# One VectorE product for both spectra in the FFT batches of an S4 and GEGLU layer, with a new order table

## The chip, the cores and the metric

The kernel runs on one core of one Trainium2 chip. The metric is the device time of one execution in microseconds (us). The time before is the median of three runs. In what follows PE is the matrix engine (TensorE) and PEld its weight loads, DVE is VectorE, ACT is ScalarE, POOL is GpSimd, SP is SyncE, which issues most DMAs.

## The reference, cut to what matters

```python
def _A_ref(u, A_re, A_im, B_re, B_im, C_re, C_im, log_dt, Dskip):
    ...
    P = jnp.exp(logdA[:, :, None] * l[None, None, :])
    K = jnp.einsum("dn,dnl,dn->dl", Cc, P, dB).real      # 448 channels, 256 states, 2048 steps
    ...
    Yf = Uf * Kf[None, :, :, :]                          # spectra of u and of K, length 4096
    y = irfft2(Yf)[..., :L]
    return y + u * Dskip

mod = (silu(c) @ w_mod)                                  # six rows: sa, ca, ga, sb, cb, gb
h = layernorm(x) * (1 + ca) + sa
x = x + ga * _A_ref(h, ...)
h = layernorm(x) * (1 + cb) + sb
x = x + gb * ((gelu(h @ w_gate) * (h @ w_up)) @ w_down)  # 448 -> 1792 -> 448
```

All inputs and the output are float32. The part that the change touches is the product of the two spectra.

## The kernel before, in words

The work falls into two halves. The first half makes the convolution kernel K, transforms u and K, multiplies the spectra and transforms back. The second half is the gated feed-forward network, in four blocks of 512 tokens.

**Making K.** The 448 channels are taken eight at a time, in 56 steps. For a step, PE makes the arguments of exponentials and of sine and cosine in PSUM (tile pg: `x.mm` line 639, `y.mm` line 658, `ang` and `anc` line 676). ACT evaluates them (`x.exp` line 645 into mx, `y.exp` line 663 into my, `mag` line 681, `sin` line 689, `cos` lines 693 and 700, into fg). DVE multiplies them into two factor tiles (`tx` line 722, 1024 elements per partition; `tyc` line 726, 2048 elements). PE contracts the factors (`kgen`, line 749, 64 small matmuls into kg). For each pair of steps `kev` copies the result out (tile ke), `kd` (line 767) adds the skip term, `ka` (line 772) does the first FFT stage, and `kout` copies that into the tile ako. `mag`, `kev`, `kout` and several other copies may be on ACT or on DVE; the order table says which for each instance. Copies on ACT have line 481, those on DVE line 483.

**The transform of u.** Four blocks of u are loaded (xt), normalised (`bn`, `norm`, `as`) and go through the first stage on PE (`ua`, line 922) to DRAM (u_d), then through the second stage (`ub`, line 985, evacuated by `ub.eg`, line 993, or `ub.ev` to tile uo) and back to DRAM (us). This runs beside the making of K.

**The product.** The channels are in three groups of 160, 160 and 128. For each of the first two groups `k_fft` runs eleven batches of three frequencies. A batch loads the spectrum of u in two arrangements into one tile (`f.ut`: ut[:, 0] is the spectrum itself, ut[:, 1] has its real and imaginary halves swapped; three DMAs, lines 1086 and 1088), loads the Fourier matrices (`f.fc`, tile fc), makes the batch's K spectrum in PSUM (`f.fwd`, line 1093, 3 matmuls of 160 columns), multiplies both arrangements by it (`f.pr`, line 1097, two operations of 3 x 160 = 480 elements each), transforms back (`f.inv`, line 1104, 6 matmuls per batch), copies out (`f.z`) and stores (`f.st`). The inverse takes the two products of a frequency in two adjacent matmuls. The third group goes through `t_fft`, with products on lines 1196 and 1199, once K is complete.

**The order.** Nothing is scheduled at run time. Every step is a task with a name and a running number, and the table PLACE gives each task one place in a single list of 2006; a letter behind a place names the engine or queue where there is a choice (a ACT, d DVE, p POOL, s SP). `Plan.run` issues the tasks in that list's order, so the table sets the order of every engine's instruction queue and of every DMA queue. Each engine works through its queue strictly in order.

The start is a chain of its own: `sil2` (lines 796 to 798) turns c into silu(c), `m.ld` loads rows of w_mod (line 806, tile fg), `m.mm` (line 816) and `m.mq0` (line 812) multiply them on PE, and the scale row for the normalisation of u (gs, line 860) needs two of them.

Of the kernel before, what the change touches and what calls it, by code (L numbers as in the profile page):

```python
# [40 lines left out]
    "anc": "127 138 148 162 173 210 218 246 266 319 327 332 359 351 433 450 484 460 499 483",  # L41
    "ang": "110 113 140 158 168 164 207 221 247 312 323 331 347 350 423 444 459 448 498 476 508 584 615 595 665 680 663 703 "
        "747 763 768 791 795 815 782 883 889 928 904 914 938 946 1012 1028 1019 1040 1045 1054 1116 1133 1142 1148 1163 "
        "1169 1175 1196",
    "as": "65d 58d 80d 105d 115d 120d 156a 146d 254d 252d 282d 296d 321a 317a 341a 353a",
    "bn": "20 45 24 40 15 17 48 16 215 216 238 245 157 220 194 190",
    "c.ai": "133",
    "c.ak": "231",
    "c.au": "47",
    "c.c": "8",  # L50
    "c.ea": "57",
    "c.ih": "516",
    "c.ld": "4",
    "c.rd": "51",
    "c.t1": "363",
    "co.adde": "1339 1352 1355 1360",
    "co.addl": "1380 1385 1420 1414",
    "co.addx": "1495 1510 1499 1522 1672 1712 1735 1684 1791 1803 1809 1801",
    "co.ca": "1400a 1406a 1446a 1439a",
    "co.cb": "1417a 1418d 1452d 1453a",  # L60
    "co.h0": "1393d 1404a 1432d 1435a",
    "co.h2": "1534a 1580a 1571a 1562a 1748a 1744d 1755a 1760d 1848d 1882a 1833a 1866a",
    "co.l0": "1408 1411 1437 1447",
    "co.l2": "1541 1585 1573 1577 1749 1751 1757 1761 1849 1885 1843 1876",
    "co.mme": "1322 1340 1335 1349",
    "co.mml": "1374 1379 1384 1387",
    "co.mmx": "1492 1506 1494 1509 1636 1699 1731 1645 1784 1797 1804 1788",
    "co.n": "1392 1403 1430 1425",
    "co.nx": "1527 1575 1549 1532 1745 1742 1747 1759 1821 1868 1829 1863",
    "co.rc": "1391 1402 1429 1424",  # L70
    "co.rcx": "1525 1739 1820",
    "co.rt": "1381 1386 1428 1422",
    "co.rtx": "1524 1737 1810",
    "co.xt": "1542 1586 1574 1578 1750 1752 1758 1762 1850 1886 1851 1877",
    "co.ta": "1398 1405 1434 1438",
    "co.tb": "1409 1415 1449 1448",
    "cos": "522 592 638 616 672 699 700 712 762 776 789 814 808 819 796 894 910 942 907 922 945 952 1016 1037 1022 1048 1060 "
        "1068 1127 1137 1153 1160 1172 1183 1207 1229",
    "cos2": "128 141 152 163 178 211 219 253 272 320 328 343 360 354 440 451 490 467 505 488",
# [3 lines left out]
    "d0": "172",  # L83
# [21 lines left out]
    "dsk": "174",  # L105
    "dt": "5",
# [4 lines left out]
    "ev.end": "1249",  # L111
    "ev.fp": "715",
    "ev.geg": "1462",
    "ev.pq": "1334",
    "ev.ps": "1433",
    "ev.ub": "397",
    "ev.w0": "1337",
    "f.fc": "724 731 767 790 810 850 871 877 918 950 964 1027 1056 1071 1098 1112 1146 1124 1202 1203",
    "f.fwd": "746 759 787 820 825 856 884 908 936 951 967 1008 1023 1039 1057 1073 1101 1126 1156 1145 1217 1214",
    "f.inv": "756 780 800 823 843 867 911 919 940 966 992 1014 1034 1051 1066 1094 1114 1131 1184 1173 1228 1225",  # L120
    "f.pr": "748 766 788 821 842 866 888 909 939 961 980 1009 1024 1043 1065 1082 1104 1130 1174 1168 1224 1221",
    "f.st": "774 827 826 891 875 901 977 960 976 997 995 1072 1062 1079 1103 1119 1121 1177 1226 1216 1260 1272",
    "f.ut": "720 758 771 794 824 855 872 899 935 916 958 993 1002 1038 1046 1070 1083 1106 1155 1115 1179 1192",
    "f.z": "757a 781a 809a 835a 869a 895d 912a 920a 965d 996a 994d 1017d 1035a 1063d 1089a 1095a 1120a 1132a 1208a 1201a "
        "1248d 1237a",
    "gs": "66 86",
# [27 lines left out]
        "1141a 1167a 1195a 1222a 1244a 1247a",  # L154
    "lt0": "64 144 325 368 560 801 861 985",
    "lt1": "92 195 326 369 723 802 968 986",
    "m.cp": "581a 600d 786a",
    "m.cp0": "50d",
    "m.ev": "44 60 63 589 619 804",
    "m.ld": "29 31 30 420 578 760",  # L160
# [251 lines left out]
def s4_geglu(ctx: ExitStack, tc: tile.TileContext, a: dict, out: bass.AP):  # L412
# [39 lines left out]
    dt, dt2 = dts_[:, :4], dts_[:, 4:]  # L452
# [1381 lines left out]
```

## Time and profile before

| | before |
|---|---|
| device time, median of 3 runs | 777.25 us (776.79 to 779.4) |
| device time of the profiled execution | 776.06 us |
| its span, first to last instruction | 774.3 us |
| granted TensorE clock | 0.995 |
| PE busy | 724.2 us (94%) |
| DVE busy | 591.3 us (76%) |
| ACT busy | 459.7 us (59%) |
| DMA traffic | 139.87 MB, mean 181 GB/s |

The span is divided into an opening of some 20 us, the making of K and the transforms up to about 340 us, a passage of some 40 us in which the third group is transformed back, and the feed-forward network from 381 us to the end. An engine's share over the whole span mixes these stages, so the busy time is read stage by stage. A row of the groups gives line, engine, operation, output <- input with shapes, count, then the summed busy time in us and the mean of one in ns, then the idle time of that engine just before them and what ended it. A row of the timeline gives the start and the length in us; the time in brackets is idle time before it.

### The profile page before, as it was taken

To read this page: it belongs to the slowest core of one execution; us is meant where nothing else is said; L and a number is where in the kernel's file an instruction comes from. 1 tells how busy PE (TensorE), PEld (TensorE's weight loads), DVE (VectorE), ACT (ScalarE), POOL (GpSimd) and SP (SyncE) were. 2 spreads that over 40 slices of the span, in tenths; PEclk is the share of its full clock that TensorE was granted. 3 is DMA by queue.
4 is the path that set the end of the run, shared out by engine and by line. 5 is a ranking of instruction groups with operands and counts; after the bars stand their busy time and mean duration, and the time that the engine had idled before them with its cause. 6 is when DMAs were issued, how large, how long until landed. Compare 5 with 4: busy or idle time off the path is not lost.

```text
span 774.3 us, 19010 instructions
## 1 busy us (share of the span) xinstructions
PE 724.2 (94%) x8166; PEld 442.5 (57%) x8166; DVE 591.3 (76%) x891; ACT 459.7 (59%) x613; POOL 8.5 (1%) x23
## 2 busy tenths in 40 slices
PE   2877889998899999989999999999999999999997
PEld 1333554443677777677874445444694446944487
DVE  6999999999999999979958932578774577144743
ACT  5899999999999999952646620244312433022330
POOL 0000000000000000003000000000000000000000
PEclk9999999999999999999999999999999999999999
DMA  9764777997888687897787791455247224013201
GB/s 265 193 187 160 214 184 222 276 272 236 247 230 252 180 233 239 275 310 208 235 269 257 221 235 79 146 166 211 98 82 211 96 96 136 14 50 99 77 2 60
DMA packets 103950, 139.87 MB, mean 181 GB/s; under 512 B 34388, under 2 KB 85492, under 8 KB 103866
## 3 DMA queue, kind: packets, MB, share of 16 engines
q1 hardware_dynamic: 100436, 132.53, 58.2%
q10 hardware_dynamic: 2950, 5.38, 2.0%
q8 instruction: 64, 1.05, 0.6%
q0 software_dynamic: 480, 0.75, 0.3%
q14 instruction: 20, 0.16, 0.1%
HBM read 100.39 MB, written 36.01 MB: 176 GB/s over the span
## 4 chain that ended last, share of the span: by engine, by line
PE 73%; ACT 12%; DVE 8%; DMA 4%; issue 2%; SPq 1%; DVEq 0%; ACTq 0%
PE pq L1530 32%; PE pq L1630 9%; PE pd L1599 4%; PE pg L676 4%; PE pf L1104 4%; PE kg L749 3%; ACT my L663 3%; DVE ty L726 2%; PE pq L1524 2%; PE pf L985 2%; PE pf L1093 2%; PE kg L772 2%; PE pf L1206 2%; ACT fg L689 2%; DMA us<-uo 2%
## 5 line engine op out<-in xcount | busy, mean ns | idle before, releaser
L1530 PE MATMUL pq<-ht,wr 128*128 128x512 f16 (+1 forms) x1200 | 248.3, 365 | 0.1
L1530 PEld LDWEIGHTS <-wr 128*128 128x128 f16 x1200 | 114.6, 98 | 128.5 <-issue 11.3
L726 DVE TENSOR_TENSOR ty<-my,fg 128x2048 f32<-128x2048 f32 x56 | 127.3, 2284 | 0.4 <-ACT fg L693 0.3
L1537 ACT ACTIVATE ge<-pq 128x512 f32<-128x512 f32 (+1 forms) x60 | 34.0, 566 | 106.9 <-PE pq L1524 71.3
L1544 DVE TENSOR_TENSOR fq<-ge,pq 128x512 f32<-128x512 f32 (+1 forms) x60 | 39.0, 650 | 72.6 <-PE pq L1530 45.0
L1556 ACT ACTIVATE hh<-fq 128x1024 f16<-128x1024 f32 (+1 forms) x49 | 46.7, 962 | 65.6 <-DVE fq L1544 47.0
L1630 PE MATMUL pq<-d,hh 128*128 128x224 f16 x476 | 68.9, 259 | 0.0
L722 DVE TENSOR_TENSOR tx<-mx,fg 128x1024 f32<-128x1024 f32 x56 | 67.6, 1218 | 0.2 <-ACT fg L700 0.2
L749 PE MATMUL kg<-ty,tx 128*32 128x64 f32 x3584 | 61.6, 222 | 4.4 <-DVE tx L722 1.7
L749 PEld LDWEIGHTS kg<-ty,tx 128*32 128x32 f32 x3584 | 53.2, 111 | 21.3 <-issue 5.9
L1559 DVE TENSOR_TENSOR hlo<-fq,hh 128x1024 f16<-128x1024 f32 (+1 forms) x49 | 53.7, 1106 | 12.9 <-ACT hh L1556 12.7
L1630 PE MATMUL pq<-d,hlo 128*128 128x224 f16 x238 | 61.6, 259 | 0.0
L689 ACT ACTIVATE fg<-pg 128x1024 f32<-128x1024 f32 x56 | 57.6, 1040 | 0.5 <-PE pg L676 0.3
L663 ACT ACTIVATE my<-pg 128x1024 f32<-128x1024 f32 x56 | 56.2, 1032 | 0.4
L1630 PEld LDWEIGHTS <-hh 128*128 128x128 f16 x560 | 54.1, 98 | 0.9 <-issue 0.2
L693 ACT ACTIVATE fg<-fg,small 128x1024 f32<-128x1024 f32 x36 | 42.2, 1180 | 0.0
L1104 PE MATMUL pf<-q,fc 128*128 128x160 f32 x264 | 41.5, 307 | 0.0
L1104 PEld LDWEIGHTS pf<-q,fc 128*128 128x128 f32 x264 | 36.5, 190 | 5.3 <-issue 2.2
L676 PEld LDWEIGHTS <-lt 64*128 64x128 bf16 x304 | 17.7, 95 | 35.0 <-issue 22.7
L676 PE MATMUL pg<-ea,lt 64*128 64x512 bf16 x152 | 31.3, 390 | 6.5 <-ACT fg L689 3.0
L1747 ACT ACTIVATE d<-fq 128x896 f16<-128x896 f32 x14 | 13.2, 946 | 39.7 <-PE pd L1599 27.3
L985 PE MATMUL pf<-ui,fu 128*128 128x448 f32 x66 | 31.2, 576 | 1.2 <-DVE uo L993 0.5
(210 smaller groups left out, 1119.2 us busy)
## 6 DMA issues: line engine op xcount, KB each, us to landing
wr<-w_d SPq DMA_DIRECT2D x21, 896.0 KB, 4.6
fc<-in_k_fc SPq DMA_DIRECT2D x20, 576.0 KB, 4.2
u_d<-so SPq DMA_DIRECT2D x32, 224.0 KB, 3.0
ui<-u_d SPq DMA_DIRECT2D x10, 672.0 KB, 6.0
fq<-in_wd SPq DMA_DIRECT2D x14, 448.0 KB, 4.1
w<-in_wgu SPq DMA_DIRECT2D x11, 512.0 KB, 4.6
us<-uo SPq DMA_DIRECT2D x22, 240.0 KB, 4.5
q<-us SPq DMA_DIRECT2D x22, 240.0 KB, 4.5
```

The costliest lines, as they stand in the source:

```text
L663: A.activation(yb.tile.rearrange("p h (n k) -> p n h k", n=2), pb.tile.rearrange("p (n h k) -> p n h k", n=2, h=2), AF.Exp)
L676: T.matmul(pa[:, nh * 512:nh * 512 + 512], w, x, start=(k == 0), stop=(k == 2))
L689: A.activation(fb.tile[:, 0].rearrange("p x (n k) -> p n x k", n=2), pb.tile.rearrange("p (n x k) -> p n x k", n=2, x=2), AF.Sin, scale=TW ...
L722: V.tensor_mul(tx.tile, xb.tile[:, xm, None, :].to_broadcast([128, 2, 512]), fb.tile[:, :, 0])
L726: V.tensor_mul(ty.tile, yb.tile[:, :, None, :].to_broadcast([128, 2, 2, 512]), fb.tile[:, None, :, 1].to_broadcast([128, 2, 2, 512]))
L749: T.matmul(kg[32 * g:32 * g + 32, 2 * (s % 2) + q, :64], tx[:, r, nh, 4 * q + g], ty[:, 0:4:3, nh, 4 * q + g] if r else ty[:, 1:3, nh, 4 * ...
L985: T.matmul(pb.tile, fu.tile[:, i], ui.tile[:, EORD[e0 + i] % 32 - s0], start=True, stop=True)
L1104: T.matmul(pz.tile[:, e % 32 - sl0], fc.tile[:, i, 1 + t], pp.tile[:, t, i], start=(t == 0 and e != 32), stop=(t == 1 and e != 0))
L1530: T.matmul(pb.tile[k][:, ts], wr.tile[:, 4 * lo + t, k, c0:c0 + 128], ht[:, m, ts], start=f % 2 == 0 and i == 0, stop=f % 2 == 1 and i == 9)
L1556: A.activation(hg.tile[0][:, cb, c], fq.tile[:, c], AF.Copy)
L1559: V.tensor_sub(hg.tile[1][:, cb, c], fq.tile[:, c], hg.tile[0][:, cb, c])
L1630: T.matmul(bank(k)[:, m], x[:, p, q[0], ts], w[:, p, q[1]], start=new and m == 0 and p == 0 and z == 0, skip_group_check=True, stop=i in ( ...
```

## The change

Line 1097 and its loop become one operation. It takes both arrangements of the spectrum of u (2 x 3 x 160 = 960 elements per partition) and reads the batch's K spectrum twice, through an access pattern that repeats it. There are 22 such batches.

```diff
         def prod():
-            for t in range(2):
-                V.tensor_mul(pp.tile[:, t, :ne], ut.tile[:, t, :ne], pk.tile[:, :ne])
+            V.tensor_mul(pp.tile[:, :, :ne], ut.tile[:, :, :ne], pk.tile[:, None, :ne].to_broadcast([128, 2, ne, n]))
```

The program is one line shorter from there on, so line 1097 becomes 1096, and every later line has a number one lower.

The rest of the change is a new table PLACE. Nearly every place up to about 1480 of the 2005 is different, most by less than ten places; the places of the feed-forward network behind it are as they were. The engine letters change too: of 16 `as` 14 instead of 11 are on DVE, of 28 `kev` 13 instead of 16, of 28 `kout` 6 instead of 7, of 36 `mag` 8 instead of 7, of 16 `ub.ev` 6 instead of 4, of 22 `f.z` 8 instead of 6, of 4 `p.e1` 4 instead of 3; the others of each are on ACT. Two lines of the table:

```diff
-    "f.pr": "748 766 788 821 842 866 888 909 939 961 980 1009 1024 1043 1065 1082 1104 1130 1174 1168 1224 1221",
+    "f.pr": "744 769 794 817 837 858 889 901 938 962 981 1004 1021 1041 1066 1076 1099 1123 1181 1148 1202 1209",
...
-    "kev": "199d 230d 290a 345a 378d 393a 462a 518d 548a 577a 654a 705a 735d 818d 805d 853d 897d 924d 969d 983d 1030d 1075d "
-        "1113d 1140a 1162a 1191a 1239d 1236a",
+    "kev": "209d 260a 290a 320a 390d 403d 420d 500a 545a 566d 683a 707a 724d 815d 799d 843a 893d 924a 971d 980a 1045d 1070d "
+        "1107a 1136a 1171a 1197a 1240d 1241a",
```

At the places that the prediction speaks of, the queues change as follows (a row of a queue gives line, operation, output <- input, size and how many follow one another; + and - mark rows of the new and of the old order). The first is SP's queue at the start of the program, where ld, c_sb, xt, fg and lh_d are the tiles that hold log_dt, c, a block of u, a row of w_mod and the scratch of the K parameters:

```order
 L487 DMA ld<-in_A_log_dt 112x4
+L512 DMA q<-in_abc 112x512
+L853 DMA xt<-in_A_u 128x1792
 L487 DMA c_sb<-in_c 112x4
-L853 DMA xt<-in_A_u 128x1792 x2
-L806 DMA fg<-in_w_mod 112x1792 x3
-L515 DMA lh_d<-in_k_one 224x512
+L806 DMA fg<-in_w_mod 112x1792 x2
+L853 DMA xt<-in_A_u 128x1792
+L515 DMA lh_d<-in_k_one 224x512
+L806 DMA fg<-in_w_mod 112x1792
```

The first two rows of w_mod now stand behind one block of u instead of two, and the third stands behind the second block.

The second is DVE's queue a little later, where the three operations of `sil2` make c_sb. Before:

```order
L549 TENSOR_TENSOR q<-q 112x256
L796 TENSOR_SCALAR sig<-sig 112x4
L797 RECIPROCAL sig<-sig 112x4
L798 TENSOR_TENSOR c_sb<-c_sb,sig 112x4
L557 TENSOR_TENSOR q<-q 112x256
```

And after:

```order
L579 TENSOR_TENSOR q<-q 112x256
L796 TENSOR_SCALAR sig<-sig 112x4
L797 RECIPROCAL sig<-sig 112x4
L798 TENSOR_TENSOR c_sb<-c_sb,sig 112x4
L583 SCALAR_TENSOR_TENSOR q<-q 112x256
L537 TENSOR_TENSOR q<-q,lh 112x512
L574 SCALAR_TENSOR_TENSOR q<-q 112x256
L575 RECIPROCAL q<-q 112x256
```

c_sb is now made behind line 579 and no longer ahead of line 557.

The third is the end of the making of K on DVE. Before:

```order
L726 TENSOR_TENSOR ty<-my,fg 128x2048
L722 TENSOR_TENSOR tx<-mx,fg 128x1024
L1097 TENSOR_TENSOR q<-q,pf 128x480 x4
L726 TENSOR_TENSOR ty<-my,fg 128x2048
L722 TENSOR_TENSOR tx<-mx,fg 128x1024
L483 COPY ke<-kg 128x4x63
L767 TENSOR_TENSOR ke<-kg,d_115 128x4 x2
L483 COPY zo<-pf 128x480
```

And after:

```order
L1096 TENSOR_TENSOR q<-q,pf 128x960
L722 TENSOR_TENSOR tx<-mx,fg 128x1024
L1096 TENSOR_TENSOR q<-q,pf 128x960
L722 TENSOR_TENSOR tx<-mx,fg 128x1024
L726 TENSOR_TENSOR ty<-my,fg 128x2048 x2
L722 TENSOR_TENSOR tx<-mx,fg 128x1024
L483 COPY ke<-kg 128x4x63
L767 TENSOR_TENSOR ke<-kg,d_115 128x4 x2
L483 COPY zo<-pf 128x320
```

The last product now has four factor operations behind it instead of two, and the last copy to zo on DVE has 320 elements instead of 480.

334 rows, old and new, of the table PLACE are left out of this document.

## The prediction

> **What bounds the kernel now.** I first read the cores and the busy time stage by stage (header, then one row per stretch of the span: PE, PEld, DVE, ACT and POOL busy with their instruction counts, the granted clock, the DMA share and rate).
>
> ```profile
> core 0: 774.3 us, clock 0.995
> ...
> core 0: us, PE busy (x) PEld busy (x) DVE busy (x) ACT busy (x) POOL busy (x), PEclk, DMA share, GB/s
> 0.00:20.00 20.00, 4.52 (x8) 2.23 (x8) 13.57 (x34) 11.22 (x19) 0.88 (x10) 1.00 0.91 266
> 20.00:60.00 40.00, 31.56 (x282) 13.62 (x280) 38.00 (x66) 37.35 (x50) 0.00 (x0) 0.96 0.72 195
> 60.00:200.00 140.00, 123.24 (x2186) 64.69 (x2184) 136.82 (x174) 137.44 (x183) 0.00 (x0) 0.99 0.78 224
> 200.00:340.00 140.00, 136.82 (x2726) 103.33 (x2726) 137.06 (x140) 133.19 (x154) 0.00 (x0) 1.00 0.82 241
> 340.00:381.00 41.00, 38.67 (x488) 32.67 (x489) 34.49 (x71) 15.97 (x34) 7.58 (x13) 1.00 0.74 218
> 381.00:774.00 393.00, 389.37 (x2482) 225.91 (x2480) 231.41 (x410) 124.49 (x177) 0.00 (x0) 1.00 0.44 134
> ```
>
> From 60 to 200 us DVE and ACT are both 98% busy and PE 88%. From 200 to 340, where the 22 batches run, PE and DVE are both 98% busy and ACT 95%. So no single engine can be relieved alone there: DVE has 3.2 us of idle time in the first of these stretches and 2.9 in the second. From 381 on PE is 99% busy and the order is nearly the old one, so the time is decided by when that stretch begins.
>
> Then DVE's waits between 60 and 345 us (waiting line, releaser, us in total, times, longest) and what the inverse transforms on PE waited for (us, times):
>
> ```profile
> DVE ke L767 <- ACT ke L481: 1.6, 2, 1.2
> DVE q L1097 <- PE pf L1093: 1.5, 3, 0.7
> ...
> DVE ty L726 <- ACT fg L693: 0.3, 1, 0.3
> ```
>
> ```profile
>   DVE q L1097: 1.5, 4
> ```
>
> All of these are small. DVE is held by its own work, with ACT and PE close behind.
>
> **The product.** The groups on DVE, and the pitch of operations that follow one another without a gap in the timeline (start, length):
>
> ```profile
> L726 DVE TENSOR_TENSOR ty<-my,fg 128x2048 f32<-128x2048 f32 x56 | 127.3, 2284 | 0.4 <-ACT fg L693 0.3
> L722 DVE TENSOR_TENSOR tx<-mx,fg 128x1024 f32<-128x1024 f32 x56 | 67.6, 1218 | 0.2 <-ACT fg L700 0.2
> ...
> L1097 DVE TENSOR_TENSOR q<-q,pf 128x480 f32<-128x480 f32 x44 | 26.5, 648 | 1.6 <-PE pf L1093 1.5
> ```
>
> ```profile
> 330.60 1.22 DVE L722 TENSOR_TENSOR tx<-mx,fg 128x1024 f32<-128x1024 f32 x1
> 331.74 2.29 DVE L726 TENSOR_TENSOR ty<-my,fg 128x2048 f32<-128x2048 f32 x1
> 333.94 1.22 DVE L722 TENSOR_TENSOR tx<-mx,fg 128x1024 f32<-128x1024 f32 x1
> 335.08 2.34 DVE L1097 TENSOR_TENSOR q<-q,pf 128x480 f32<-128x480 f32 x4
> 337.33 2.29 DVE L726 TENSOR_TENSOR ty<-my,fg 128x2048 f32<-128x2048 f32 x1
> 339.54 1.22 DVE L722 TENSOR_TENSOR tx<-mx,fg 128x1024 f32<-128x1024 f32 x1
> ```
>
> By the means, an element costs (1218 - 648) / 544 = 1.05 ns and an operation has a fixed part of 648 - 480 x 1.05 = 145 ns. But each operation starts 0.08 us before the one ahead of it ends (331.74 + 2.29 = 334.03, the next at 333.94), so that part is paid only in part. Four products take 337.33 - 335.08 = 2.25 us, 0.563 each; 1024 elements take 1.14, 2048 take 2.20, so an element costs (2.20 - 1.14) / 1024 = 1.035 ns. A product of 960 then takes 0.563 + 480 x 0.001035 = 1.06 against 1.125 for two: 0.065 us saved, times 22 batches = 1.4 us of DVE time. The bounds are 0 (the repeated read is no faster than two operations) and 22 x 0.145 = 3.2 (the whole fixed part). I take 1.4: the timeline has the pitch of this very operation, and the factor tile of line 726, which is built from two repeated reads, shows no extra price.
>
> The Trainium skill would put it higher. Its page Perfetto Trace Analysis (Optimizing Scalar/DVE Operations) gives a Vector instruction about 125 ns of overhead on PSUM, 60 on SBUF, and advises grouping when the engine is saturated; as an estimate from that page, 22 x 0.125 = 2.75 us. The pitch above, with one operand in PSUM, agrees with the lower figure, and the measurement decides. The page VectorE: DVE Perf Modes (The DRAIN you can't avoid) says that a next operation waits until the pipe is empty, by which the saving would be the upper bound; the starts above come before the end, so the trace speaks against it here.
>
> The merged operation must wait for all three loads of the batch and for the K spectrum at once; the next factor operations are queued behind it on DVE, and the inverse behind it on PE. The loads cost nothing: no DMA stands among the waits of line 1097. The inverse needs both products from its second matmul on, so its start moves by less than one product, 0.56, and only in the four batches where PE waited: at worst 4 x 0.56 = 2.2 us of PE waits, and I take 0, since the second half also ends 0.065 earlier.
>
> The Trainium skill has a rule against such merging in the same section of Perfetto Trace Analysis: where Vector isn't saturated but makes others wait, smaller instructions may finish work sooner. The trace has DVE at 98% there, so the rule's condition isn't met.
>
> **The moved copies.** The engine letters move work between ACT and DVE. Rows on DVE, then three of their counterparts on ACT:
>
> ```profile
> L684 DVE TENSOR_SCALAR fg<-pg 128x1024 int32<-128x1024 int32 x7 | 8.5, 1218 | 0.3 <-PE pg L676 0.3
> L483 DVE COPY ke<-kg 128x252 f32<-128x252 f32 x16 | 6.6, 412 | 0.6 <-PE kg L749 0.6
> L483 DVE COPY ako<-kg 128x512 f32<-128x512 f32 x7 | 4.8, 683 | 0.0
> L483 DVE COPY zo<-pf 128x480 f32<-128x480 f32 x6 | 3.9, 650 | 0.0
> L483 DVE CAST lh<-q 112x512 bf16<-112x512 f32 x9 | 3.8, 418 | 0.1
> L912 DVE TENSOR_SCALAR as<-au,rs 128x128 f32<-128x128 f32 x11 | 3.0, 281 | 0.2
> L483 DVE COPY uo<-pf 128x448 f32<-128x448 f32 x4 | 2.5, 620 | 0.2 <-DMA us<-uo 0.2
> ```
>
> ```profile
> L681 ACT ACTIVATE fg<-pg 128x1024 f32<-128x1024 f32 x29 | 30.2, 1044 | 0.1
> L481 ACT ACTIVATE ke<-kg 128x252 f32<-128x252 f32 x12 | 4.8, 404 | 5.1 <-PE kg L749 5.1
> L910 ACT ACTIVATE as<-au,rs 128x128 f32<-128x128 f32 x5 | 2.0, 400 | 0.0
> ```
>
> Each counted at its mean less the 0.08 overlap, and up to the last factor operation: DVE gains one `mag` (+1.14), three `as` (+0.60), one cast to lh (+0.34), two copies to uo (+1.08) and two of 480 to zo (+1.14; one stood behind the last factor before), and loses three to ke (-1.0) and one to ako (-0.6). That is +2.7 us, and with the merge DVE's work up to its last factor is 2.7 - 1.4 = +1.3 us. ACT's rows are about as long, so I take it as 2.7 us lighter. I count DVE's +1.3 in full, since DVE has almost no idle time, and set against it what ACT's relief can give back: DVE waits on ACT for about 2 us in the list above; I take 1.0 of it (bounds 0 and 2.7).
>
> **The opening.** SP's queue, PE's first matmul, the step that makes c_sb, the row that stood ahead of the new place of it, and the scale row that ends this chain on ACT; then the size of one block of u:
>
> ```profile
> 2.62 0.90 SPq L853 DMA_DIRECT2D xt<-in_A_u  x2
> 3.56 2.28 SPq L806 DMA_DIRECT2D fg<-in_w_mod  x3
> ```
>
> ```profile
> 15.48 4.97 PE L816 MATMUL pf<-fg,c_sb 112*128 112x448 f32 x8 [15.48 <-DVE q L574]
> ```
>
> ```profile
> 8.02 0.16 DVE L798 TENSOR_TENSOR c_sb<-c_sb,sig 112x4 f32<-112x4 f32 x1
> ...
> 13.16 0.43 DVE L579 TENSOR_TENSOR q<-q 112x256 f32<-112x256 f32 x1
> ```
>
> ```profile
> 24.58 0.54 ACT L834 ACTIVATE gs<-pf 128x448 f32<-128x448 f32 x1 [1.42 <-PE pf L816]
> ```
>
> ```profile
> xt<-in_A_u SPq DMA_DIRECT2D x4, 896.0 KB
> ```
>
> The first matmul names DVE as its releaser, but c_sb was done at 8.2; what came at 15.5 must be the first row of w_mod, which stood behind two blocks of u. One block less is 0.92 MB / 266 GB/s = 3.4 us sooner. Then c_sb is the later one: behind line 579 and its three short steps it is ready at about 13.16 + 0.35 + 0.5 = 14.0. So PE starts up to 1.4 us sooner. The scale row needs the third row of w_mod as well, whose place behind the same bytes is unchanged, so I take half, 0.7 (bounds 0 and 1.4).
>
> **The rest.** SP issues the same DMAs in another order; the passage from 340 to 381 has PE 94% busy with unchanged work, so I take 0 there, with 2.3 us (its PE idle time) as the bound to either side.
>
> The sum: +1.3 - 1.0 - 0.7 = -0.4 us against the profiled execution's own 776.06 (span 774.3 and 1.8 around it). The median of the runs is 1.2 above that execution, so the forecast for the median is 777.25 - 0.4 = 776.9. A measurement of this kernel can tell about 0.3%, 2.3 us, from no change.
>
> **The rivals.**
>
> Faster: ACT, not DVE, sets the pace up to 200 us. For it: ACT is the busiest there (137.44 of 140), and PE, 88% busy, would take up the batches as soon as they can start. Then ACT's 2.7 us come off in full, with 0.7 from the opening: 777.25 - 3.4 = 773.9. Against it: DVE has only 3.2 us of idle time there, and its own work grows.
>
> Slower: the ledger of DVE alone decides. The merged operation takes as long as two, ACT's relief and the opening give nothing, and the moved copies are paid in full: 777.25 + 2.7 = 780.0. It decides from a pitch of the merged operation of about 1.11 us on (2.7 less 22 x 0.015 is 2.3). For it: DVE's 98%. Against it: the pitches of lines 722 and 726.
>
> That the change doesn't do what it says can be left out: the new queue of DVE holds 22 operations of 960 elements and none of 480.
>
> **How the numbers follow.** The forecast, no measurable change, gets 0.42, the faster rival 0.32, the slower 0.26; a new order of some 1480 steps can lose or win small waits anywhere, which keeps the two rivals high. The range reaches past both: to 773.9 less the other half of the opening and as much of the passage (0.7 each), 772.5, and to 780.0 plus 1.0 of the PE waits priced above, 781.0.
>
> **What would show it.** In the profile after: line 1096 x22 with a mean near 1.14 us (1.06 and the overlap of 0.08) and a pitch of 1.06; DVE still 97% busy or more from 60 to 340 with ACT some 2 to 3 us lighter up to the last exponentials; PE's first matmul near 14; the last factor operation on DVE within 2 us of 339.5. The prediction is wrong if the last factor moves by more than 2.3 us, if line 1096 waits for DMAs, or if the passage of 41 us changes by more than 2.

## The result and the profile after

The changed kernel is slower. Over two sets of runs its median is 785.8 us (four runs, 782.6 to 790.1) and 784.2 us (six runs, 783.2 to 787.1), against 778.1 and 778.6 for the kernel before beside them: ratios 1.010 (95% interval 1.0068 to 1.0132) and 1.0081 (1.0062 to 1.0100). The prediction, 776.9 with a range of 772.5 to 781.0, is wrong in sign and size. The profiled execution took 784.24 us, with a span of 782.5 us, 8.2 more than before. The medians differ by less, 7.7 and 5.6 us; the profiled execution of the kernel before, 776.06, is faster than all four of its runs beside the changed kernel (776.79 to 779.4).

The same views as before, first the cores and the busy time by stretch:

```profile
core 0: 782.5 us, clock 0.993
...
0.00:20.00 20.00, 4.67 (x7) 2.21 (x8) 11.86 (x30) 10.88 (x18) 0.81 (x10) 1.00 0.92 228
20.00:60.00 40.00, 29.68 (x191) 12.29 (x190) 32.49 (x61) 31.35 (x42) 0.00 (x0) 0.87 0.64 180
60.00:200.00 140.00, 123.05 (x2122) 63.65 (x2119) 136.58 (x178) 135.12 (x179) 0.00 (x0) 1.00 0.76 221
200.00:340.00 140.00, 134.46 (x2662) 101.32 (x2663) 137.07 (x123) 133.69 (x154) 0.00 (x0) 1.00 0.82 238
340.00:381.00 41.00, 38.34 (x634) 32.70 (x632) 35.12 (x53) 17.65 (x31) 6.26 (x11) 1.00 0.77 232
```

The second row is the one to read. Between 20 and 60 us DVE worked 32.49 us instead of 38.00 and ACT 31.35 instead of 37.35, and the granted clock was 0.87 instead of 0.96. Behind 60 us the rows look like those of before. So the opening comes first. Its rows on SP's queue, PE, DVE and ACT (a view each; the columns are start, length, and in brackets the idle time before):

```profile
3.09 0.97 SPq L806 DMA_DIRECT2D fg<-in_w_mod  x2
4.11 0.68 SPq L853 DMA_DIRECT2D xt<-in_A_u  x1
4.82 0.80 SPq L515 DMA_DIRECT2D lh_d<-in_k_one  x1
5.67 0.75 SPq L806 DMA_DIRECT2D fg<-in_w_mod  x1
```

```profile
15.33 6.34 PE L816 MATMUL pf<-fg,c_sb 112*128 112x448 f32 x8 [15.33 <-DVE c_sb L798]
21.61 1.01 PE L812 MATMUL pf<-fg,c_sb 112*32 112x448 f32 x8
24.74 4.94 PE L816 MATMUL pf<-fg,c_sb 112*128 112x448 f32 x8 [2.12 <-ACT rs L887]
```

```profile
11.46 0.63 DVE L878 BATCH_NORM_STATS2 st<-xt 128x6 f32<-128x448 f32 x1 [2.91 <-DMA xt<-in_A_u]
...
14.40 0.39 DVE L579 TENSOR_TENSOR q<-q 112x256 f32<-112x256 f32 x1
...
15.12 0.16 DVE L798 TENSOR_TENSOR c_sb<-c_sb,sig 112x4 f32<-112x4 f32 x1
```

```profile
29.71 0.55 ACT L834 ACTIVATE gs<-pf 128x448 f32<-128x448 f32 x1 [3.88 <-PE pf L816]
```

The third group of w_mod matmuls in the kernel before, for comparison:

```profile
21.27 3.27 PE L816 MATMUL pf<-fg,c_sb 112*128 112x448 f32 x8
```

c_sb was ready at 15.12 + 0.16 = 15.3 and not at 14.0, because the statistics of the first block of u (line 878) stand ahead of it on DVE's queue and waited 2.91 us for that block. PE therefore began at 15.33, as late as before (15.48). Then it did what it had not done before: it stood idle for 2.12 us ahead of the third group of w_mod matmuls. The row names ACT, but what the group reads is the third row of w_mod. The trace records when each load has landed, and the third row landed at 24.6 us, against 20.5 before; in other profiles below the same wait is put down to that load. The third group then took 4.94 us, where the same 8 matmuls took 3.27 before. So the scale row started at 29.71 and not at 24.58: 24.74 - 21.27 = 3.5 us because the third group started later, and 4.94 - 3.27 = 1.7 because it took longer.

The granted clock in slices of 5 us, of the changed kernel and of the kernel before (columns as above, the clock third from the end):

```profile
25.00:30.00 5.00, 5.00 (x10) 2.25 (x9) 2.23 (x4) 1.07 (x3) 0.00 (x0) 0.66 0.62 166
30.00:35.00 5.00, 3.50 (x19) 1.45 (x19) 4.29 (x8) 4.76 (x6) 0.00 (x0) 1.00 0.65 168
35.00:40.00 5.00, 3.32 (x19) 1.29 (x17) 5.00 (x12) 4.26 (x8) 0.00 (x0) 0.88 0.64 173
40.00:45.00 5.00, 3.98 (x16) 1.23 (x13) 4.96 (x14) 4.20 (x7) 0.00 (x0) 0.77 0.58 162
45.00:50.00 5.00, 4.07 (x18) 1.86 (x18) 2.51 (x5) 4.33 (x5) 0.00 (x0) 0.66 0.68 179
```

```profile
25.00:30.00 5.00, 3.92 (x21) 1.73 (x21) 4.40 (x9) 4.76 (x6) 0.00 (x0) 1.00 0.86 218
30.00:35.00 5.00, 3.34 (x18) 1.20 (x17) 4.93 (x11) 4.86 (x9) 0.00 (x0) 0.76 0.99 259
35.00:40.00 5.00, 4.19 (x20) 1.30 (x17) 4.52 (x12) 4.94 (x6) 0.00 (x0) 0.90 0.02 6
40.00:45.00 5.00, 3.58 (x43) 1.74 (x44) 4.91 (x7) 4.95 (x6) 0.00 (x0) 1.00 0.89 229
```

Before, (0.24 + 0.10) x 5 = 1.7 us of clock were lost in these slices; after, (0.34 + 0.12 + 0.23 + 0.34) x 5 = 5.15. The first of the losses falls on the third group. The kernel before has one more such dip behind these slices, from 59.9 to 63.3 us, so up to the fifth factor operation (below) it is 3.4 against 5.1.

The product itself (its group, two starts of the timeline, and its waits between 60 and 345 us):

```profile
L1096 DVE TENSOR_TENSOR q<-q,pf 128x960 f32<-128x960 f32 x22 | 25.3, 1150 | 2.2 <-PE pf L1093 2.2
```

```profile
329.24 1.15 DVE L1096 TENSOR_TENSOR q<-q,pf 128x960 f32<-128x960 f32 x1
330.30 0.16 DVE L767 TENSOR_TENSOR ke<-kg,d 128x4 f32<-128x4 f32 x1
```

```profile
DVE q L1096 <- PE pf L1093: 2.2, 5, 0.9
```

Its pitch is 330.30 - 329.24 = 1.06 us and its mean 1.15, as forecast. It waits 2.2 us for the K spectrum, where the two operations waited 1.5, and for no DMA.

The end of it, the first gate and up matmul, of before and of after:

```profile
380.80 1.47 PE L1530 MATMUL pq<-ht,wr 128*128 128x256 f16 x12
```

```profile
388.99 1.25 PE L1529 MATMUL pq<-ht,wr 128*128 128x256 f16 x10
```

It starts 8.2 us later, and the span is 8.2 us longer: the feed-forward network adds nothing. To have the loss by stages, I take the stretch between the ends of the fifth and of the last factor operation of line 722 (one row of busy time over just that stretch; kernel before, then after):

```profile
65.23:340.76 275.53, 255.50 (x4832) 165.25 (x4828) 269.45 (x305) 265.43 (x330) 0.00 (x0) 1.00 0.80 231
```

```profile
70.87:348.35 277.48, 257.35 (x4834) 167.10 (x4833) 271.19 (x294) 264.88 (x328) 0.00 (x0) 1.00 0.79 231
```

So of the 8.2 us, 70.87 - 65.23 = 5.6 are made ahead of the fifth factor, 277.48 - 275.53 = 2.0 in the steady stretch, and the remaining 0.6 in the passage.

### The profile page after: what moved, and what is told of

Read it like the earlier page. It is cut to its first block, busy times and chain, and to the rows that moved or that the text cites. A ratio compares the mean times of both kernels' runs of the same rounds, so it can differ in the third digit from the quotient of the medians.

```text
span 782.5 us, 18984 instructions
## 1 busy us (share of the span) xinstructions
PE 727.6 (93%) x8166; PEld 444.6 (57%) x8166; DVE 591.6 (76%) x873; ACT 458.8 (59%) x609; POOL 8.5 (1%) x23
## 4 chain that ended last, share of the span: by engine, by line
PE 50%; DMA 1%; DVE 1%; ACT 1%; ACTq 0%; issue 0%; SPq 0%
PE pq L1529 31%; PE pq L1629 9%; PE pd L1598 4%; PE pq L1523 2%; PE pd L1629 2%; PE pd L1403 1%; DMA my<-in_k_ft 1%; DVE my L1198 1%; DMA w<-in_wgu 0%; PE pd L1408 0%; DMA y<-lh 0%; PE pd L1689 0%; PE pq L1689 0%; PE pd L1469 0%; ACTq L1331 0%
## 5 line engine op out<-in xcount | busy, mean ns | idle before, releaser
L749 PEld LDWEIGHTS kg<-ty,tx 128*32 128x32 f32 x3584 | 52.8, 110 | 21.5 <-issue 13.2
L772 PE MATMUL kg<-ak,ke 128*64 128x128 f32 x448 | 30.2, 278 | 1.5 <-DVE ke L767 1.5
```

Source lines behind the costliest of these rows:

```text
L749: T.matmul(kg[32 * g:32 * g + 32, 2 * (s % 2) + q, :64], tx[:, r, nh, 4 * q + g], ty[:, 0:4:3, nh, 4 * q + g] if r else ty[:, 1:3, nh, 4 * ...
```

## The experiments

**Theories.** Theory 1: the loss is made in the opening, by the new order of the loads (PE waits for the third row, the clock falls). Theory 2: the new order or the moved copies lose it in the steady stretch. Theory 3: the merged operation costs it, by its waits. In the texts on record, "the kernel with the merged product alone" is the first of the following. All tables are edited as a list of places, so the diffs show a few of the places that change.

**The merged product in the old order, and the new order with two products.**

```diff
 # old PLACE
-            for t in range(2):
-                V.tensor_mul(pp.tile[:, t, :ne], ut.tile[:, t, :ne], pk.tile[:, :ne])
+            V.tensor_mul(pp.tile[:, :, :ne], ut.tile[:, :, :ne], pk.tile[:, None, :ne].to_broadcast([128, 2, ne, n]))
```

> The merged product in the old order. Theory 1 (the loss is made in the opening by the new order): the time stays within 2.3 us of the kernel before, 777 +- 1.5, the gain being at most 22 x 0.065 = 1.4 us; the scale row on ACT (line 834) starts at 24.6 +- 0.5 and the last factor operation ends at 340.8 -1.4 / +0.5. Theory 2 (the steady stretch from 60 to 340 loses by the new order): the same. Theory 3 (the merged operation costs by its waits): about 785, with the loss between 200 and 340 us.

```diff
 # new PLACE
-            V.tensor_mul(pp.tile[:, :, :ne], ut.tile[:, :, :ne], pk.tile[:, None, :ne].to_broadcast([128, 2, ne, n]))
+            for t in range(2):
+                V.tensor_mul(pp.tile[:, t, :ne], ut.tile[:, t, :ne], pk.tile[:, :ne])
```

> The new order with the product as two operations of 480 elements. Theory 1 and theory 2: 785.8 + 1.4 = 787 +- 1.5, with the scale row at 29.7 +- 0.7 by theory 1. Theory 3: about 778, as the kernel before.

The merged product alone: 777.8 us, ratio 0.9991 (0.998 to 1.0002). The order alone: 783.6, ratio 1.0077 (1.0051 to 1.0102). Theory 3 falls; the order is the loss. The steady stretch of the merged product alone shows where its gain went:

```profile
66.41:342.14 275.73, 256.57 (x4830) 166.41 (x4827) 268.26 (x283) 265.73 (x330) 0.00 (x0) 0.99 0.80 231
```

DVE is busy for 268.26 us instead of 269.45, 1.2 less, close to the 1.4 of the forecast. But the stretch is as long as before (275.73 to 275.53): DVE's idle time grew from 275.53 - 269.45 = 6.1 to 7.5. In this profile the gain turned into waiting. The time leaves more room: a ratio of 0.998, the lower end of its interval, would be a gain of 1.6 us.

**Half of the order at a time.** The first 130 places as before, and the reverse.

```diff
-    "m.ld": "28 37 29 449 599 756",
+    "m.ld": "29 31 30 449 599 756",
-    "x.ld": "30 13 212 153",
+    "x.ld": "19 10 214 155",
```

> The merged product and the new order, but the first 130 places hold the old tasks in the old order (up to about 50 us). Theory 1: 778 +- 1.5, at least 6 us below the changed kernel, with the scale row at 24.6 +- 0.5 and a last factor operation that ends within 2 us of 341. Theory 2: 785 +- 1.5, with the opening as before and the loss made after 60 us. Theory 3: 785, lost where the products run.

```diff
-    "pad": "34 228 503 812",
+    "pad": "34 134 261 750",
-    "x.ld": "30 13 212 153",
+    "x.ld": "30 13 215 143",
```

> The merged product, the first 133 places of the new order and the old order behind them. Theory 1: 785 +- 1.5, with the scale row at 29.7 +- 0.7. Theory 2: 778 +- 1.5. Theory 3: 785.

The old opening: 780.2, ratio 1.0024 (1.0010 to 1.0038). The new opening with the old rest: 781.4, ratio 1.0039 (1.0022 to 1.0057). Neither theory 1 nor theory 2 alone is right: each half loses something. Against the merged product alone (0.9991) the opening costs 0.48%, 3.7 us, and the rest 0.33%, 2.6 us. The steady stretch with the old opening and the new rest:

```profile
65.45:343.25 277.80, 257.52 (x4832) 167.73 (x4828) 271.21 (x293) 264.13 (x327) 0.00 (x0) 0.99 0.79 230
```

It is 2.1 longer than that of the merged product alone, and DVE is busy for 2.95 us more. With the new opening and the old rest it is 275.5.

The new opening has a surprise in its profile: its third group waits, but isn't slow.

```profile
21.42 3.24 PE L816 MATMUL pf<-fg,c_sb 112*128 112x448 f32 x8 [1.74 <-DMA fg<-in_w_mod]
```

**The opening, taken apart.** The changed kernel once more, without an edit; with the third row requested earlier; with PE kept busy in the wait; with 68 old places.

> The changed kernel once more, on the chip of the three next ones. The four runs so far spread from 782.6 to 790.1. Expected: a median of 785 +- 2 against 778 for the kernel before. If its spread comes from the opening, the profile shows the third group of w_mod matmuls (line 816) starting at 21 to 25 us after a wait of 1.7 to 2.1 us, either with the granted clock down in the 5 us around it (group of 4.9 us) or not (3.3 us).

```diff
-    "m.ld": "28 37 29 449 599 756",
+    "m.ld": "28 30 29 449 599 756",
-    "x.ld": "30 13 212 153",
+    "x.ld": "31 13 212 153",
```

> The changed kernel with the third row of w_mod requested right behind the second, ahead of the second block of u and of the pad. Theory 1 (the new order of the loads makes PE wait for the third row, and the clock falls in that wait): PE goes from the second to the third group of line 816 without a wait, the group takes 3.3 us, the scale row (line 834, second start) is 3 to 5 us sooner, and the time is 3 to 5 us below the changed kernel. Theory 2 (the opening does not matter, the order of the rest does): the time is the changed kernel's, within 1.

```diff
-                for t in range(4):
+                for t in list(range(4)) * (1 if deps[2:] else 3):
                     T.matmul(pb.tile[32 * t:32 * t + 32], c_sb[:, t:t + 1].to_broadcast([DT, 32]), wb.tile[:, t],
```

> The changed kernel with the small matmuls of line 812 done three times over (the same result again), so that PE works on through most of the wait for the third row. The row comes no sooner. Theory 1a (the idle time itself costs, through the granted clock): the clock stays at 1.00 through the third group, which takes 3.3 us and not 4.9, and the time is about 1.7 to 3 us below the changed kernel. Theory 1b (only the lateness of the row costs): the same time as the changed kernel, or up to 0.5 above.

```diff
-    "gs": "63 84",
+    "gs": "66 84",
-    "m.ld": "28 37 29 449 599 756",
+    "m.ld": "29 31 30 449 599 756",
```

> The changed kernel with its first 68 places (about 30 us) as in the old order. Theory 1: the scale row starts as in the kernel before (24.6 +- 0.5, by the second start of line 834) and the time is that of the kernel with 130 old places, 780 +- 1. If the places from 68 to 130 matter as well, it lies between that and the changed kernel, at 782 to 784.

The changed kernel again: 784.2 us. The third row first: 785.6, ratio 1.0099 (1.0074 to 1.0125), no gain, against theory 1 in this form. PE did go on without a wait, as expected, but now the second block of u came later, and ACT's queue held the scale row up behind a step that needs that block. It still came sooner, at 26.25 us for 28.12 and 29.71 in the two profiles of the changed kernel:

```profile
25.12 0.30 ACT L887 ACTIVATE rs<-mv,small 128x8 f32<-128x8 f32 x1 [3.96 <-DVE mv L879]
...
26.25 0.52 ACT L834 ACTIVATE gs<-pf 128x448 f32<-128x448 f32 x1
```

PE, done with its third group at 23.5, now had its wait behind that group, 2.80 us ahead of line 823. The clock then stayed at half from 28.7 to 42.4 us, the longest dip in any of the openings, and the first factor operation ended 22.2 us behind the scale row instead of 19.8:

```profile
30.00:35.00 5.00, 5.00 (x19) 2.32 (x17) 3.00 (x7) 2.13 (x3) 0.00 (x0) 0.50 0.71 196
```

PE kept busy: 787.8, ratio 1.0102 (1.0059 to 1.0144), with runs from 780.1 to 791.2. On the time it tells little: its runs scatter over 11 us, and the profiled one is the slowest. They fall into two groups, two runs of 780.1 and 780.9 us with a mean clock of 0.996 and 0.995, and four of 786.6 to 791.2 with 0.984 to 0.989: in one and the same program the time goes with the clock. On the third group it tells what it was made for, since the row came at 22.55 and the group ran at full clock:

```profile
19.91 2.46 PE L812 MATMUL pf<-fg,c_sb 112*32 112x448 f32 x24
22.55 3.24 PE L816 MATMUL pf<-fg,c_sb 112*128 112x448 f32 x8 [0.18 <-DMA fg<-in_w_mod]
```

68 old places: 781.8, ratio 1.0055 (1.0033 to 1.0077). That is 0.26 to 0.45% below the two results of the changed kernel, while 130 old places (1.0024) take 0.57 to 0.76% away.

**The loads alone, and the first 68 places alone.**

```diff
-    "m.ld": "28 37 29 449 599 756",
+    "m.ld": "29 34 30 449 599 756",
-    "pad": "34 228 503 812",
+    "pad": "37 228 503 812",
-    "x.ld": "30 13 212 153",
+    "x.ld": "28 13 212 153",
```

> The changed kernel with only the six loads of the start in the old order on SP's queue (two blocks of u, three rows of w_mod, the pad), all else as changed. Theory 1 (the late third row of w_mod makes the loss of the opening): the third group of line 816 starts without a wait at 21.5 +- 0.7, takes 3.3 us, the scale row starts by 25 and the time is 3 to 4 below the changed kernel, 781 +- 1. Theory 1c (the order of the other engines in the opening, with c_sb made late and the second block's statistics ahead, makes it): 784 to 785, as the changed kernel.

```diff
 # old PLACE but for the first 68 places
-    "m.ld": "29 31 30 420 578 760",
+    "m.ld": "28 37 29 420 578 760",
-    "x.ld": "19 10 214 139",
+    "x.ld": "30 13 214 140",
```

> The merged product in the old order, with only the first 68 places (about 30 us) as in the new one. In the profiles so far it takes 17.8 us from the scale row (line 834) to the end of the first factor operation with the old order behind place 68, and 19.8 with the new. If the places up to 68 make the loss of the opening (the third row's wait and the low clock behind it): about 2 to 3.5 above the kernel with the merged product alone (777.8), 780 to 781. If the places from 68 to 133 make it: 778 +- 1, with 17.8 +- 0.5 from the scale row to the first factor.

The old loads in the changed kernel: 782.3, ratio 1.0043 (1.0029 to 1.0058). With six DMAs moved and nothing else, 0.38 to 0.57% of the loss is gone (1.0081 and 1.010, less 1.0043). As expected the third group follows without a wait:

```profile
23.70 3.27 PE L816 MATMUL pf<-fg,c_sb 112*128 112x448 f32 x8
```

It starts at 23.7, not at the 21.5 expected: the first row came at 18.0 in this run, and the third landed at 23.2, no sooner than in the changed kernel, run again (23.0). So what this profile gained is not an earlier row but a third group at full clock, and fewer dips behind it. Its eight runs have a mean clock of 0.994, the changed kernel's ten 0.990. The first 68 places alone bring the loss back: 781.9, ratio 1.0048 (1.0025 to 1.0071), with a third group that starts at 24.98 after 2.72 us of waiting and takes 4.85. From the scale row to the first factor it takes 19.3 us here and 19.7 with 68 old places and new ones behind, for 17.8 with 130 old ones: either part of the new order stretches it, and which step does was not taken apart.

The openings of these runs side by side, each from one profile; "loads" says whether the six loads of the start are in the old or the new order, and the landing is the trace's record of it:

| kernel | loads | third row landed | wait ahead of third group, its start, its length | scale row | from it to the first factor's end | clock lost in dips that begin between 18 us and there |
|---|---|---|---|---|---|---|
| before | old | 20.5 | none, 21.27, 3.27 | 24.6 | 17.8 | 1.7 |
| merged product alone | old | 22.2 | none, 22.46, 3.27 | 25.8 | 17.8 | 1.7 |
| 130 old places | old | 19.9 | none, 21.43, 3.27 | 24.7 | 17.8 | 1.7 |
| 68 old places | old | 20.2 | none, 22.79, 3.27 | 26.1 | 19.7 | 3.4 |
| changed, old loads | old | 23.2 | none, 23.70, 3.27 | 27.0 | 19.1 | 1.7 |
| 133 new places | new | 21.3 | 1.74, 21.42, 3.24 | 24.7 | 19.8 | 3.4 |
| order alone | new | 23.1 | 1.92, 23.21, 4.86 | 28.1 | 19.8 | 5.1 |
| changed, again | new | 23.0 | 2.00, 23.17, 4.92 | 28.1 | 19.8 | 5.1 |
| changed | new | 24.6 | 2.12, 24.74, 4.94 | 29.7 | 19.8 | 5.1 |
| 68 new places | new | 24.8 | 2.72, 24.98, 4.85 | 29.9 | 19.3 | 6.8 |
| PE kept busy | new | 22.4 | 0.18, 22.55, 3.24 | 25.8 | 19.8 | 3.4 |
| third row first | third row moved up | 20.1 | none, 20.25, 3.24 | 26.3 | 22.2 | 8.5 |

Two things repeat. No profile with the old loads waits ahead of the third group, and every one with the new loads does, though only for 0.18 us where PE is given other work. And a wait of 1.92 us or more goes with a third group that takes 4.85 to 4.94 us, one of 1.74 or less with 3.24. How early the third row arrives is another matter. With the old loads it lands from 19.9 to 23.2 and its group starts from 21.3 to 23.7; with the new ones it lands from 21.3 to 24.8. So it tends to come later with the new loads, but the two ranges overlap, and the profile that I compared with at first, that of the kernel before, has the earliest start of those with the old loads.

**The steady stretch: letters or order?** The old engine letters with 130 old places and the new order, the new letters in the old order, and fewer magnitudes on DVE in the old order.

```diff
-    "as": "65d 58d 80d 105d 115d 120d 152d 180d 251d 258d 271d 277d 285a 319d 328d 355d",
+    "as": "65d 58d 80d 105d 115d 120d 152a 180d 251d 258d 271d 277d 285a 319a 328a 355a",
```

> The kernel with 130 old places, and on top of that the old engine letters everywhere (same list of places). Theory A (the copies that the letters moved to DVE make the loss between 60 and 340 us, ACT's relief gives nothing back): from the fifth to the last factor operation of line 722 it takes 275.7 +- 0.6 as with the old order, not 277.8, and the time is 778 +- 1, some 2 below the kernel with 130 old places (780.2). Theory B (the new order of the tasks makes it): 277.8 +- 0.6 there and 780 +- 1.

```diff
-    "as": "65d 58d 80d 105d 115d 120d 156a 146d 254d 252d 282d 296d 321a 317a 341a 353a",
+    "as": "65a 58d 80d 105d 115d 120d 156d 146d 254d 252d 282d 296d 321a 317d 341d 353d",
```

> The old order and the merged product, with the new engine letters alone. Theory A: DVE is 3 us busier and the stretch from the fifth to the last factor operation takes 277.8 +- 0.6; time 780 +- 1, some 2 above the kernel with the merged product alone (777.8). Theory B: 275.7 +- 0.6 and 778 +- 1.

```diff
-    "mag": "511a 591a 617a 598d 670d 689a 668a 708a 752d 764a 770a 792a 797d 816a 784a 892a 890d 929a 905a 915a 943a 947a "
+    "mag": "511a 591a 617a 598d 670a 689a 668a 708a 752d 764a 770a 792a 797a 816a 784a 892a 890d 929a 905a 915a 943a 947a "
```

> The old order and the merged product, with three of the seven magnitudes on DVE (line 684, 1.22 us each) moved to ACT (line 681, 1.04 each). Theory A (DVE's work sets the stretch, ACT has room): 3 x 1.14 = 3.4 us come off DVE, the stretch takes 2 to 3.4 less than 275.7, and the time is 775 +- 1. Theory C (DVE and ACT set it together, either way of moving work loses or gives nothing): 275.7 +- 0.6 or longer, time 777.8 +- 1 or more.

Old letters in the new order: 802.0, ratio 1.0284 (1.0256 to 1.0312). New letters in the old order: 793.2, ratio 1.0181 (1.0160 to 1.0201). Neither theory A nor theory B had this: letters and order belong together, and mixing them costs 15 to 22 us whichever way. The busy time shows that it isn't work that was added (old letters in the new order, its stretch):

```profile
68.40:356.60 288.20, 257.54 (x4832) 166.50 (x4828) 269.32 (x289) 267.32 (x332) 0.00 (x0) 1.00 0.77 223
```

DVE is busy for 269.32 us, less than with the changed kernel, and idle for 18.9. The stretch has 10.4 of the 22 us; another 10 stand behind the last factor operation, where the letters of the copies of the third group (`t.z`, `t.z0`, `co.cb`) changed as well. Three magnitudes less on DVE: 780.9, ratio 1.0019 (1.0002 to 1.0035), slower and not faster:

```profile
67.61:345.69 278.08, 257.17 (x4832) 167.31 (x4828) 265.65 (x280) 268.50 (x333) 0.00 (x0) 0.99 0.79 229
```

DVE has 2.6 us less to do than with the merged product alone and waits 4.9 us longer (278.08 - 265.65 = 12.4, for 7.5). Theory A, the ledger of DVE, fails as a rule: taking this work off DVE doesn't shorten the stretch in this order. Theory C's numbers came out. But only three magnitudes were moved, with every place left as it was, so this doesn't show that no lighter DVE would help.

**Where in the new order the stretch is lost.** The new order from place 130 up to place 350, 560 or 740, the old one around it.

```diff
 # e.g. up to 740, against the changed kernel
-    "gs": "63 84",
+    "gs": "66 86",
-    "pad": "34 228 503 812",
+    "pad": "35 100 503 750",
```

> Old order up to place 130, new order to 350 (about 97 us), old order behind, merged product. The kernel with the new order from 130 to the end stood 2 us ahead of the old order at the ninth factor (94.0 for 96.0) and lost 4 between the 17th and the 29th. If that lead is real progress: 776 +- 1. If it is only factors done ahead of other work: 778 +- 1.

> The same with the new order to place 560 (about 145 us). If the loss of the steady stretch is made where the batches begin (behind place 560): 776 to 778, and 275.7 or less from the fifth to the last factor operation. If it is made ahead of it: 780 and 277.8.

> The same with the new order to place 740, behind which the 22 batches stand (about 195 us). If the loss comes with the batches: 776 to 778 and 275.7 or less from the fifth to the last factor. If it is made between places 560 and 740, where both orders finish the second stage of the transform of u: 780 and 277.8, unlike the cut at 560.

To 350: 779.0, ratio 1.0009 (0.9992 to 1.0025), stretch 275.6. To 560: 783.4, ratio 1.0058 (1.0038 to 1.0079), stretch 279.8. To 740: 779.3, ratio 1.0005 (0.9986 to 1.0023), and this stretch:

```profile
66.70:343.00 276.30, 256.73 (x4834) 165.98 (x4830) 270.26 (x294) 264.56 (x326) 0.00 (x0) 1.00 0.79 231
```

The lead at the ninth factor was no progress: kept to place 350 it gives nothing. The cut at 560 makes a loss of its own at its seam, larger than that of the whole new order, and tells nothing else. The cut at 740 leaves 276.3 - 275.7 = 0.6 of the 2.1 us, so by the traces 1.5 us are lost behind place 740, where the batches run. In time the cut at 740 and the 130 old places (1.0024) differ by no more than their intervals, so this place of the loss rests on one profile each. That the new order behind place 130 costs the stretch some 2 us repeats: it takes 277.2 to 279.0 us in six profiles (the changed kernel twice, the order alone, 130 and 68 old places, the old loads) and 274.4 to 275.7 in the four with the old order there (before, the merged product alone, 133 and 68 new places). The third row first has 281.6 and PE kept busy 287.8, with mean clocks of 0.983 and 0.985 over these executions. Whether it is the order or the letters behind place 740 stays open, as the two can't be taken apart.

## Why the prediction was wrong, point by point

- **The opening** is the step that failed most. It said: "The scale row needs the third row of w_mod as well, whose place behind the same bytes is unchanged, so I take half, 0.7 (bounds 0 and 1.4)." The place was not unchanged: in the new queue the load of lh_d (224 KB), which stood behind the third row, stands ahead of it. And the row did land later, from 21.3 to 24.8 us in the six profiles with the new loads, from 19.9 to 22.2 in the ten that begin with the old order's first 68 places. The order of the loads isn't all of that, since the changed kernel with the old loads had it at 23.2. The step also had no term for what PE does until then. Before, PE started late, behind two blocks of u, and its first two groups lasted until the third row was there. In the new order PE has two rows early and then waits 1.74 to 2.72 us for the third. In four of five profiles that wait was followed by a third group of 4.9 us instead of 3.3, 1.6 us on the chain to the scale row, and by more slices at a low clock up to the first factor (5.1 to 6.8 us of clock lost against 1.7). In time the opening costs 3.7 us instead of giving 0.7.
- **The first row** was forecast 3.4 us sooner, for one block of u less ahead of it. It landed at 15.1 us instead of 15.3 in the pair of profiles, and at 12.6 to 15.1 in the six with the new loads, for 15.3 to 17.6 in the ten. The forecast had the transfers at 266 GB/s throughout; in the changed kernel's first 20 us they moved 228.
- **The clock over the whole run.** The mean granted clock was 0.990 over the changed kernel's ten runs (0.986 to 0.993) and 0.995 over the runs of the kernel before. The difference, before rounding, is 0.0043; of 727.6 us of busy PE that is 3.1 us, about half of the loss, the opening's dips among it. This is an estimate, and a high one, as it counts every microsecond at half clock as if PE held the kernel up. With 130 old places the mean is 0.995 and with the old loads 0.994, so the fall goes with the new opening; with 68 old places it is 0.992. I had read the clock in the profile of before as constant, and no bound of mine had it.
- **Why the third row first didn't mend it:** the scale row came 1.9 to 3.5 us sooner, though it waited on ACT behind the second block of u. But PE's wait only moved, to 2.80 us behind the third group, and the half clock that followed lasted for 13.65 us. As I read it, all six loads are needed before the chain ends, so the order can only choose who waits; the old order lets PE wait at the start, where it has nothing to lose. Why the dip was so long stays open.
- **c_sb** at 14.0 was 1.3 too early in the forecast: I added the three short steps to the time at which line 579 ran before. Four statistics of u stand ahead of line 579 in both orders, and in the new one they wait for the first block, which landed at 11.4 us and not at 9.1. In the old loads' run c_sb was ready 4.4 us ahead of PE's start, so by itself it costs nothing.
- **The product:** pitch 1.06 and mean 1.15, as forecast; DVE's work fell by 1.2 us of the 1.4. But none of it showed in the stretch, 275.7 with it and 275.5 without, and in time the gain is 0.7 us with an interval from -0.2 to 1.6. The saving on DVE was right and its worth is not shown, because I let DVE's work count in full.
- **The moved copies:** +2.7 forecast for DVE, +2.95 measured (merged product alone against 130 old places). ACT was lighter by 265.73 - 264.13 = 1.6, not 2.7.
- **ACT's relief,** -1.0 in the sum, gave nothing: DVE's idle time in the stretch was 6.1 us before and 277.48 - 271.19 = 6.3 after. The stretch grew by 2.0, where the terms had +1.3 - 1.0 = +0.3. That was close to the slower rival's number, 2.7, but not to its reason: the merged operation was not slow, and the work of DVE alone doesn't set the stretch, as three magnitudes less show. (Where that rival begins to hold, 2.7 less 22 x 0.015 is 2.4 and not 2.3; nothing hangs on it.) What the stretch lost was lost behind place 130, by the traces mostly behind place 740; which steps there lose it stays open.
- **The passage and the feed-forward network** were as said: +0.6, within the bound of 2.3, and 0.

The signs that I named did show it: the last factor moved by 7.6 us, not by less than 2, and PE's first matmul came at 15.3, not near 14. The range was too narrow by what it left out, a bound for the opening on the side of a loss: I had bounded that term at 0 and -1.4, with no reason that excluded a later scale row.

## What to carry to other kernels

When loads at the start are put in another order, follow the engine that consumes them up to the last load, not to the first: an early start that ends in a wait can be worth less than a late start without one. Put a bound on the side of a loss on every term whose order changes, and a term for the granted clock wherever the change gives PE an idle stretch of some microseconds. When two orders are compared, count every transfer ahead of the one that matters, small ones too. Where two engines are both over 95% busy and their queues were ordered together, busy time saved on one of them is not yet time saved: here 1.2 us of it became waiting in the profile, and work moved in either direction made the stretch longer.

## What the runs showed of the hardware

The clock falls in units. Slices of half a microsecond of the changed kernel, at the first dip and at the start of the two others:

```profile
25.00:25.50 0.50, 0.50 (x2) 0.31 (x2) 0.50 (x2) 0.46 (x2) 0.00 (x0) 0.69 0.51 197
25.50:26.00 0.50, 0.50 (x2) 0.09 (x2) 0.50 (x1) 0.33 (x1) 0.00 (x0) 0.50 0.24 90
...
28.50:29.00 0.50, 0.50 (x2) 0.19 (x2) 0.00 (x0) 0.00 (x0) 0.00 (x0) 0.89 1.02 290
38.50:39.00 0.50, 0.50 (x4) 0.27 (x6) 0.50 (x3) 0.50 (x2) 0.00 (x0) 0.85 0.85 265
45.50:46.00 0.50, 0.24 (x2) 0.13 (x3) 0.32 (x1) 0.50 (x2) 0.00 (x0) 0.67 0.00 0
```

In these records the clock is full or half. A slice at 0.69 was at half clock for 0.31 / 0.5 of its 0.5 us, so the first dip lasts from 25.2 to 28.6, 3.4 us, and the others start at 38.85 and 45.7: 13.7 and 6.8 later, multiples of 3.4 again. The clock lost in the table of the openings goes in steps of 1.7 in the same way. The Trainium skill's page TensorE: Matmul & The Clock Gate (What's actually happening) says that a free-running window of about 3.4 us decides between half and full clock; the dips here agree. Its advice to avoid idle gaps over about 3 us (Why this matters for your kernels) is too loose for this case: gaps of 1.92 to 2.72 us, between two groups of matmuls, were followed by a dip, one of 1.74 was not. By the traces they differ in where the gap falls in the steps of 3.41 us. PE was busy for 0.88 to 1.63 of the 3.41 us just ahead of the four dips. The kernel with 133 new places, whose steps are counted back from its first dip at 38.1, has its gap across the end of such a step, and PE was busy for 2.07 us in it. First the step ahead of the changed kernel's first dip, then that one:

```profile
21.78:25.19 3.41, 1.29 (x9) 0.32 (x6) 3.21 (x11) 2.50 (x4) 0.00 (x0) 1.00 0.95 325
17.61:21.02 3.41, 2.07 (x11) 0.43 (x10) 3.27 (x9) 2.24 (x3) 0.00 (x0) 1.00 1.02 319
```

Busy time alone gives no rule: with the third row first, the step from 21.87 to 25.28 has 1.62 us of it and no dip behind it. That the position of the gap changes from run to run would explain why the changed kernel varies by 7.5 us (782.6 to 790.1), but the profiles, one execution each, don't show it.

The clock column reads 1.00 at the start, though the traces have no record of the clock there. The first record of the clock begins at 18.97 us in the kernel before and at 21.78 in the changed one. Until then the matmuls of the first group ran at half pace: in the kernel before they took up to 1.09 us each, where those at full clock took 0.54. So the same 8 matmuls took 4.97 us at the start of the kernel before and 6.34 in the changed one, and the sums of lost clock above leave this part out.
